# An FNet mixing and GEGLU pair on Trainium2: keeping the sums of eleven more matrix tiles between the two mixings

## The chip, the cores and the metric

The kernel runs on one core of a Trainium2 chip. The metric is the device time of one launch in microseconds (us). The kernel before takes 1598.94 us, the median of three runs between 1597.33 and 1599.78 us.

## The reference

A matrix x of 2048 rows and 512 columns (float32) passes through four residual layers: mixing, GEGLU, mixing, GEGLU. `_layernorm` has no learned weights.

```python
def _A_ref(x, dft_seq_re, dft_seq_im, dft_hid_re, dft_hid_im):
    a = jnp.einsum("bsd,ed->bse", x, dft_hid_re)
    b = jnp.einsum("bsd,ed->bse", x, dft_hid_im)
    y = jnp.einsum("ts,bse->bte", dft_seq_re, a) - jnp.einsum("ts,bse->bte", dft_seq_im, b)
    return y

def _B_ref(x, w_gate, w_up, w_down):
    return (_gelu(x @ w_gate) * (x @ w_up)) @ w_down

x = x + _A_ref(_layernorm(x, axis=-1), A_dft_seq_re, A_dft_seq_im, A_dft_hid_re, A_dft_hid_im)
x = x + _B_ref(_layernorm(x, axis=-1), B_w_gate, B_w_up, B_w_down)
x = x + _A_ref(_layernorm(x, axis=-1), A_dft_seq_re, A_dft_seq_im, A_dft_hid_re, A_dft_hid_im)
x = x + _B_ref(_layernorm(x, axis=-1), B_w_gate, B_w_up, B_w_down)
```

Both mixings use the same sequence matrices (2048 x 2048, real and imaginary), so whatever is computed from these matrices alone is the same in layer 0 and in layer 2.

## The kernel before

**Products.** Each float32 operand is split into two parts that TensorE (PE) takes: `split` (lines 156 to 160) lets ScalarE (ACT) write the rounded copy `hi` (L158) and VectorE (DVE) the rest `lo` (L160). `mm3` (lines 213 to 217) then makes three matmuls of 128x128 by 128x512: hi with hi (L215), hi with lo (L216), lo with hi (L217). To need fewer of them, the kernel multiplies 2x2 blocks by a scheme with seven products in place of eight, and such a scheme multiplies sums of blocks. For the sequence matrices the blocks of a step k are the tiles a11, a12, a21 and a22, 128x512 each (256 KB), and the sums are S1 = a21 + a22, S3 = a11 - a21, S2 = S1 - a11 and S4 = a12 - S2, by `minus` (L191) and `plus` (L198) on DVE.

**Stages.** A mixing (`mix`) treats the matrix rows in four blocks b = 0 to 3. First come the stages A11 and A12 of all blocks. Then each block has its stage S2, which runs the products of S2, S1 and S3 over the eight steps k, with S1 one step and S3 two steps behind S2 (`skewed`), then a few products with the hidden matrices, its stage S4 with the products of A22 and S4, and the rest of the hidden products. In layer 2 the blocks 2 and 3 use another form of the hidden products (`PAIRED`, tiles `wq`). The GEGLU of layer 1 follows, in two halves w, and layer 2 and 3 go the same way. The weights of the GEGLUs (`wb`, `wc`) are prepared beside the first mixing and stored to HBM by GpSimd (POOL).

**The stream of matrix tiles.** `mix_items` (lines 518 to 557) lists for every use of a matrix tile the addresses to load and the function that makes its two parts. `take` (line 356) hands the next parts to the products; `split_next` and `load_next` (lines 331 to 354) keep up to seven items split ahead and four more loaded ahead. Loads go out on SyncE's (SP's) DMA queue (L338), stores on POOL's queue. All tiles live in 98 slots of 256 KB that are handed out in the order in which they came free; a load into a slot waits until its last reader, and any store out of it, is done.

**Sums that are kept.** In layer 0 the sums of some (b, k) are stored to HBM as they are made, and in layer 2 loaded in place of the raw tiles. `KEPT` (line 50) lists which: steps 0, 1 and 2 of block 0. Two more, steps 0 and 1 of block 3, are computed and stored during layer 1 (`summed_ahead`, `SUMMED = 2`). The store is in `sums_kept`, the load in `mix_items`:

```python
def sums_kept(layer, at, sums):
    if layer == 0 and at in KEPT:
        for i, v in sums.items():
            nc.gpsimd.dma_start(wss[at][i], v)
...
for i, k in skewed(3):
    if layer and (b, k) in wss:
        raw(plain, wss[b, k][i])
    elif i == 0:
        raw(make_s2(layer, b, k), a21[k], a22[k], *(() if hold else (a11[k],)))
    else:
        raw(make_s1(k) if i == 1 else make_s3(k))
```

A step that isn't kept loads three raw tiles in stage S2 and makes three sums of them on DVE; S1 and S3 stay in their slots until their turn comes. In stage S4 it loads a12 and makes S4. A kept step loads S2, S1, S3 and S4 one by one, four tiles as well, and only splits them.

**Order.** Each engine runs its instructions in order. A scheduler orders them by a simulated timeline when the program is built, so a change at one place moves its neighbours on all engines.

Of the kernel before, what the change touches and what calls it, by code (L numbers as in the profile page):

```python
# [46 lines left out]
LATER = 3  # L47
LET = 5
SUMMED = 2
KEPT = ((0, 0), (0, 1), (0, 2))  # L50
DOWN_RUNS = ((0,0,0,0),(4,4,4,0),(4,4,4,0),2)


# [1 line left out]
def fnet_geglu(ctx: ExitStack, tc: tile.TileContext, x_in, ws, wh, wgu, wdn, wdc, whc, out):  # L55
# [240 lines left out]
    def fetched(key):  # L296
# [9 lines left out]
        (b, k): [dram.tile([P, 512], F32, name=f"ws{b}_{k}_{i}") for i in range(4)]  # L306
        for b, k in [*KEPT, *((NB - 1, k) for k in range(SUMMED))]
    }
# [87 lines left out]
# [4 lines that stand above are left out]
# [1393 lines left out]
```

## Time and profile before

| what | value |
|---|---|
| median of three runs | 1598.94 us |
| time of the profiled execution | 1598.04 us |
| span of the profiled execution | 1596.3 us |
| PE busy | 1589.5 us, 100% of the span |
| DVE busy | 1169.6 us, 73% |
| ACT busy | 891.8 us, 56% |
| POOL busy | 293.4 us, 18% |
| moved by DMA | 431.75 MB, mean 270 GB/s |

The span runs from the first to the last instruction of the profiled execution; 1.7 us of its time lie around it. Layer 0 ends at about 405 us, layer 1 at about 804 us, layer 2 at about 1174 us. In the rows of groups stand the line, the engine, the operation, the tiles written and read, the count, the busy time and the mean duration, and then the idle time of the engine just before them.

### The profile page before, as it was taken

To read this page: it belongs to the slowest core of one execution; us is meant where nothing else is said; L and a number is where in the kernel's file an instruction comes from. 1 tells how busy PE (TensorE), PEld (TensorE's weight loads), DVE (VectorE), ACT (ScalarE), POOL (GpSimd) and SP (SyncE) were. 2 spreads that over 40 slices of the span, in tenths; PEclk is the share of its full clock that TensorE was granted. 3 is DMA by queue.
4 is the path that set the end of the run, shared out by engine and by line. 5 is a ranking of instruction groups with operands and counts; after the bars stand their busy time and mean duration, and the time that the engine had idled before them with its cause. 6 is when DMAs were issued, how large, how long until landed. Compare 5 with 4: busy or idle time off the path is not lost.

```text
span 1596.3 us, 22839 instructions
## 1 busy us (share of the span) xinstructions
PE 1589.5 (100%) x6984; PEld 1310.4 (82%) x6984; DVE 1169.6 (73%) x2030; ACT 891.8 (56%) x1731; POOL 293.4 (18%) x505
## 2 busy tenths in 40 slices
PE   9999999999999999999999999999999999999999
PEld 6888888888888888888888888888878888888887
DVE  7998878888689794665879767778895557744574
ACT  8955465754767553566657535566453565333460
POOL 4122111242456101330040000011301000000000
PEclk9999999999999999999999999999999999999999
DMA  9888888997998999997895876877978958895445
GB/s 359 289 330 316 289 316 282 351 308 210 328 322 316 286 320 284 339 364 240 282 307 178 271 252 212 283 233 251 256 255 279 276 183 253 298 285 181 133 145 158
DMA packets 244058, 431.75 MB, mean 270 GB/s; under 512 B 29344, under 2 KB 68512, under 8 KB 242912
## 3 DMA queue, kind: packets, MB, share of 16 engines
q1 hardware_dynamic: 214128, 337.21, 66.0%
q0 software_dynamic: 27120, 90.99, 16.0%
q10 hardware_dynamic: 2688, 2.10, 0.4%
q8 instruction: 55, 0.90, 0.2%
q14 instruction: 67, 0.55, 0.1%
HBM read 341.31 MB, written 88.87 MB: 269 GB/s over the span
## 4 chain that ended last, share of the span: by engine, by line
PE 93%; issue 2%; DMA 2%; DVE 1%; POOL 1%; ACT 0%; SPq 0%; DVEq 0%; POOLq 0%; ACTq 0%
PE p L217 31%; PE p L216 31%; PE p L215 31%; DVE s L160 1%; DMA s<-t 1%; PE p L1016 1%; DVE s L191 0%; POOL rstd L634 0%; DMA s<-wb 0%; DMA s<-x 0%; POOL s L760 0%; DMA s<-wq 0%; DVE s L195 0%; ACT s L158 0%; POOL wb L324 0%
## 5 line engine op out<-in xcount | busy, mean ns | idle before, releaser
L216 PE MATMUL p<-s,s 128*128 128x512 f32 x2312 | 897.4, 389 | 0.4 <-DVE s L160 0.4
L217 PE MATMUL p<-s,s 128*128 128x512 f32 x2312 | 891.9, 389 | 0.3 <-DMA s<-wb 0.3
L215 PE MATMUL p<-s,s 128*128 128x512 f32 x2312 | 860.4, 389 | 0.3 <-ACT p L209 0.2
L158 ACT ACTIVATE s<-s 128x512 fp32r<-128x512 f32 (+1 forms) x855 | 481.1, 607 | 262.2 <-DVE s L191 67.7
L160 DVE TENSOR_TENSOR s<-s,s 128x512 fp32r<-128x512 f32 (+1 forms) x855 | 537.2, 663 | 114.4 <-ACT s L158 95.2
L215 PEld LDWEIGHTS p<-s,s 128*128 128x128 f32 x2312 | 434.0, 188 | 91.8 <-ACT p L209 0.9
L216 PEld LDWEIGHTS p<-s,s 128*128 128x128 f32 x2312 | 434.0, 188 | 91.2 <-DVE s L160 1.1
L217 PEld LDWEIGHTS p<-s,s 128*128 128x128 f32 x2312 | 434.0, 188 | 91.0 <-DMA s<-wb 0.8
L195 DVE TENSOR_TENSOR s<-s,p 128x512 f32<-128x512 f32 x201 | 135.9, 683 | 160.6 <-PE p L217 139.8
L191 DVE TENSOR_TENSOR s<-s,s 128x512 f32<-128x512 f32 (+1 forms) x413 | 243.9, 611 | 5.7 <-DMA s<-ws 3.3
L202 ACT ACTIVATE s<-p 128x512 f32<-128x512 f32 x232 | 134.5, 593 | 111.2 <-PE p L217 109.1
L1270 ACT ACTIVATE s<-s 128x512 f32<-128x512 f32 x84 | 52.8, 628 | 45.8 <-DVE s L195 45.5
L1270 ACT ACTIVATE s<-p 128x512 f32<-128x512 f32 x28 | 16.7, 598 | 84.1 <-PE p L217 82.4
L324 POOL DMA_DIRECT2D wb<-s x84 | 46.1, 550 | 90.7 <-ACT s L158 67.8
L634 POOL TENSOR_SCALAR rstd<-rstd 128x1 f32<-128x1 f32 x40 | 18.2, 455 | 237.9 <-ACT s L633 230.0
L160 DVE TENSOR_TENSOR s<-xwide,s 128x512 fp32r<-128x512 f32 (+1 forms) x52 | 34.8, 679 | 30.6 <-ACT s L158 30.6
L657 ACT ACTIVATE s<-s,shift,rstd 128x512 f32<-128x512 f32 x59 | 47.5, 811 | 14.6 <-DVE shift L624 8.1
L1286 DVE TENSOR_TENSOR s<-s,p 128x512 f32<-128x512 f32 x56 | 38.3, 684 | 23.4 <-PE p L217 23.4
L198 DVE TENSOR_TENSOR s<-s,s 128x512 f32<-128x512 f32 (+1 forms) x71 | 42.9, 611 | 13.1 <-DMA s<-ws 11.0
L209 ACT ACTIVATE p<-p 128x512 f32<-128x512 f32 x56 | 32.6, 584 | 24.7 <-PE p L217 24.4
L158 ACT ACTIVATE s<-xwide 128x512 fp32r<-128x512 f32 (+1 forms) x52 | 31.6, 622 | 25.7 <-DVE xwide L195 18.3
L1207 POOL DMA_DIRECT2D wc<-s x42 | 30.5, 728 | 70.2 <-ACT s L158 61.3
(104 smaller groups left out, 613.3 us busy)
## 6 DMA issues: line engine op xcount, KB each, us to landing
s<-ws SPq DMA_DIRECT2D x404, 256.0 KB, 5.2
s<-wb SPq DMA_DIRECT2D x294, 256.0 KB, 5.1
s<-wc SPq DMA_DIRECT2D x182, 256.0 KB, 4.5
wb<-s POOLq DMA_DIRECT2D x98, 256.0 KB, 4.9
s<-wh SPq DMA_DIRECT2D x84, 256.0 KB, 5.4
s<-x SPq DMA_DIRECT2D x55, 256.0 KB, 5.3
wc<-s POOLq DMA_DIRECT2D x49, 256.0 KB, 5.3
xwide<-ws SPq DMA_DIRECT2D x37, 256.0 KB, 5.4
```

The source lines that it names most:

```text
L158: newest["ACT"] = nc.scalar.activation(hi, src, AF.Copy)
L160: newest["DVE"] = nc.vector.tensor_tensor(lo, src, f32(hi), op=ALU.subtract)
L191: nc.vector.tensor_tensor(out, a, b, op=ALU.subtract)
L195: bank_read["DVE"] = nc.vector.tensor_tensor(out, a, b, op=ALU.add)
L198: nc.vector.tensor_tensor(out, a, b, op=ALU.add)
L202: bank_read["ACT"] = nc.scalar.activation(v, src, AF.Copy)
L215: nc.tensor.matmul(ps, ah, bh, start=start, stop=False, skip_group_check=True)
L216: nc.tensor.matmul(ps, ah, bl, start=False, stop=False, skip_group_check=True)
L217: newest["PE"] = nc.tensor.matmul(ps, al, bh, start=False, stop=stop, skip_group_check=True)
L324: nc.gpsimd.dma_start(a, f32(t))
L657: nc.scalar.activation(z, x, AF.Identity, bias=shift, scale=rstd)
L1270: nc.scalar.activation(t, g, AF.Gelu_apprx_tanh)
```

## The change

`KEPT` gets eleven more pairs (b, k): steps 0, 2, 4 and 6 of block 1, the same of block 2, and steps 2, 4 and 6 of block 3.

```diff
-KEPT = ((0, 0), (0, 1), (0, 2))
+KEPT = tuple((b, k) for b, ks in enumerate(((0, 1, 2), (0, 2, 4, 6), (0, 2, 4, 6), (2, 4, 6))) for k in ks)
```

In layer 0, 44 more stores of 256 KB go out on POOL's queue (L399); there the sums are made as before. In layer 2, 44 sums on DVE are no longer made, and 44 loads on SP's queue read a stored sum in place of a raw tile. The scheduler puts the instructions around them in another order.

The first place is POOL's queue at the end of block 2 and in stage S2 of block 3 of layer 0. `ws` with block, sum and step behind it is a stored sum (L399), `x_2` an output of the mixing (L285), `t_0_0` and `t_0_1` the transposed input of layer 1 (L760 fetches a part of it). Before:

```order
L285 DMA x_2_90<-s_3963 128x512
L1210 DMA wb_153<-s_3954 128x512
L285 DMA x_2_90<-s_3966 128x512
L760 DMA xwide<-t_0_0_2598 32x4x128 x4
L760 DMA s_4259<-t_0_0_2598 32x4x128
L760 DMA s_4187<-t_0_1_2599 32x4x128 x4
```

After:

```order
L399 DMA ws_4_0_177<-s_3990 128x512
L285 DMA x_2_90<-xwide 128x512
L285 DMA x_2_90<-s_4039 128x512
L285 DMA x_2_90<-s_4042 128x512
L285 DMA x_2_90<-s_4045 128x512
L399 DMA ws_2_1_174<-s_3847 128x512
L399 DMA ws_2_2_175<-s_3845 128x512
L760 DMA xwide<-t_0_0_2656 32x4x128 x4
L399 DMA ws_2_0_173<-s_3849 128x512
L760 DMA s_4306<-t_0_1_2657 32x4x128 x4
L760 DMA s_4344<-t_0_0_2656 32x4x128 x4
```

The fetches of `t_0_0` and `t_0_1` stood together behind the outputs; now stores of block 3's sums stand ahead of them and between them. Block 3 has twelve such stores: three ahead of the outputs of block 2, nine between these and the end of the fetches' stretch.

The second place is SP's queue ahead of stage S2 of block 3 in layer 2. `ws` without numbers is a raw matrix tile, `ws_2_0` and the like are stored sums (step, sum). Before:

```order
L338 DMA s_12325<-ws 128x512
L338 DMA s_12323<-ws 128x512
L338 DMA s_12327<-ws 128x512
L338 DMA s_12333<-ws_1_1_146 128x512
L338 DMA s_12364<-ws 128x512
L338 DMA s_12368<-ws 128x512
L338 DMA s_12366<-ws 128x512
L338 DMA s_12411<-ws_1_2_147 128x512
```

After:

```order
L338 DMA s_12380<-ws_2_0_173 128x512
L338 DMA s_12386<-ws_1_1_190 128x512
L338 DMA s_12392<-ws_0_2_187 128x512
L338 DMA s_12417<-ws 128x512
L338 DMA s_12421<-ws 128x512
L338 DMA s_12419<-ws 128x512
L338 DMA s_12451<-ws_2_1_174 128x512
L338 DMA s_12463<-ws_1_2_191 128x512
```

Step 2 loaded three raw tiles at once for its sums; now it loads S2 alone at that place, and S1 and S3 each follow some loads later.

## The prediction

> **What bounds the kernel now.** I read the page first, then busy times by stretch, then who waited for whom. The page's first lines say that TensorE is the bound:
>
> ```profile
> span 1596.3 us, 22839 instructions
> ...
> PE 1589.5 (100%) x6984; PEld 1310.4 (82%) x6984; DVE 1169.6 (73%) x2030; ACT 891.8 (56%) x1731; POOL 293.4 (18%) x505
> ...
> PEclk9999999999999999999999999999999999999999
> ```
>
> A busy PE need not be PE at its pace, since matmuls overlap, so the pace itself has to come from a stretch in which nothing held it up. The view of busy times in five stretches (the start, and layers 0 to 3) gives it; behind PE's busy time stands the number of matmuls, and the last three numbers are the clock, the share of the DMA engines and GB/s:
>
> ```profile
> 20.00:405.00 385.00, 385.00 (x1700) 318.75 (x1698) 324.69 (x575) 240.60 (x471) 99.49 (x168) 1.00 0.88 301
> 405.00:804.00 399.00, 398.91 (x1761) 330.10 (x1760) 297.89 (x521) 243.76 (x486) 114.19 (x185) 1.00 0.92 309
> 804.00:1174.00 370.00, 369.02 (x1626) 304.66 (x1625) 287.62 (x513) 209.19 (x408) 51.67 (x94) 1.00 0.79 251
> 1174.00:1596.30 422.30, 418.53 (x1845) 345.78 (x1843) 245.84 (x384) 184.53 (x346) 17.85 (x34) 1.00 0.72 220
> ```
>
> In layer 0 PE is busy in all of 385.00 us and does 1700 matmuls: 385.00/1700 = 0.2265 us each. At this pace the 1626 matmuls of the third row need 368.3 us of 370.0 (1.7 us lost), the 1761 of the second 398.8 us of 399.0 (0.2 us), the 1845 of the last 417.9 us of the 418.5 in which PE ran (0.6 us; the rest of that row is the end after the last matmul). So all that any change outside the start can win is 1.7 + 0.2 + 0.6 = 2.5 us, or 0.16% of 1598.94 us. The change leaves the count of matmuls, and the start, as they are. I take 0.2%, 3.2 us, as the least that a measurement of this kernel tells from no change: its three runs lie 2.45 us apart. A gain that can be told is therefore shut out by the rows, unless by a stray run.
>
> PE's own waits after the start are three, as the view of who waited for whom has them:
>
> ```profile
> PE p L216 <- DVE s L160: 0.4, 1, 0.4
> PE p L217 <- DMA s<-wb: 0.3, 1, 0.3
> PE p L215 <- ACT p L209: 0.2, 1, 0.2
> ```
>
> The latter two are the end of layer 2, where the timeline of PE shows them:
>
> ```profile
> 1167.14 0.39 PE L216 MATMUL p<-s,s 128*128 128x512 f32 x1
> 1167.86 0.50 PE L217 MATMUL p<-s,s 128*128 128x512 f32 x1 [0.33 <-DMA s<-wb]
> ...
> 1168.90 0.62 PE L215 MATMUL p<-s,s 128*128 128x512 f32 x2
> 1169.73 0.50 PE L215 MATMUL p<-s,s 128*128 128x512 f32 x1 [0.21 <-ACT p L209]
> ```
>
> From 1167.14 to 1167.86 PE does one matmul in 0.72 us, 0.49 more than its pace; from 1168.90 to 1169.73 two in 0.83 us, 0.38 more.
>
> **The change part by part: layer 2.** The 44 sums that go cost DVE what this row of groups says (L198, the pluses, has the same mean):
>
> ```profile
> L191 DVE TENSOR_TENSOR s<-s,s 128x512 f32<-128x512 f32 (+1 forms) x413 | 243.9, 611 | 5.7 <-DMA s<-ws 3.3 <-PE p L216 0.7
> ```
>
> 44 x 0.611 = 26.9 us of DVE's 287.6 in layer 2. Nearly all of that lies beside PE, which loses 1.7 us in the whole layer, so its worth is what it does at the two waits that DVE has a hand in. One is the wait for DVE L160, in stage S2 of block 0, where DVE itself is behind. Block 0's kept steps stay 0, 1 and 2, so I cost this at nothing and leave its wait where it is. The other is the wait for `wb` at 1167.86. The chain of waits leads to it through DVE:
>
> ```profile
> 1148.88 0.92 DVE s L191 x2
> ...
> 1159.77 0.60 DVE s L191
> ...
> 1161.60 0.60 DVE s L191
> 1162.20 0.28 DVE s L160
> 1162.48 5.34 DMA s<-wb
> ```
>
> DVE works without a break from 1148.88 to 1162.48, and the load of the weights starts when it is done (a slot comes free). In stage S4 of block 3 three of these subtractions go (steps 2, 4 and 6), 3 x 0.611 = 1.8 us, and nine sums went in the stage S2 just ahead. The load then starts at least 1.8 us earlier, and 0.49 us is all it has to make up. So this wait goes: -0.49 us. Next is the wait for ACT L209 behind it, a copy from one PSUM bank to another between two products; it hangs on PE's own last product and not on DVE. The bounds are 0 and -0.38; I take -0.1, nearer to no change.
>
> The loads of layer 2 stay as many, four tiles for a step, but S1 and S3 come from HBM where they lay in a slot. What a late load does is shown by the wait rows: ACT stood 19.6 us in 17 waits for matrix tiles, up to 3.8 us at once, while PE has only the one wait for a split, 0.4 us, which the sentence above ties to DVE:
>
> ```profile
> ACT s L158 <- DMA s<-ws: 19.6, 17, 3.8
> ```
>
> So up to 3.8 us of lateness at the split is hidden by the parts made ahead, and the cost is 0, with an upper bound that I take with layer 0's below.
>
> **Layer 0.** Here 44 stores are added. The twelve of block 0 in this trace give their price on POOL:
>
> ```profile
> L399 POOL DMA_DIRECT2D ws<-s x9: 539/539/542, 81.2 to 95.1; - x9
> DMA to landing us min/median/max: 5.3/6.9/7.8
> ```
>
> 44 x 0.539 = 23.7 us of POOL, which is busy in 99.5 of 385 us: hidden. What queues behind a store that waits for its sum are POOL's steps of the layer norms (L634, L635), for which ACT waits, and the fetches L760. The first row here is from the view of who waited for whom, the second from the chain of waits:
>
> ```profile
> ACT shift L636 <- POOL rstd L635: 16.4, 13, 4.9
> 361.80 18.56 issue
> ```
>
> ACT stood up to 4.9 us there, and PE has no wait for it in its three. The last of the added stores stand ahead of the 18.56 us in which the chain only passes time until POOL's next store. So I cost the queue at 0, between 0 and the 0.5 us by which a late ACT already delays PE at the end of layer 0.
>
> The bytes are the open cost. 44 x 262,144 = 11.5 MB go into layer 0. The stretches of its last two blocks, in the view of busy times:
>
> ```profile
> 254.00:287.00 33.00, 33.00 (x148) 27.32 (x147) 28.44 (x50) 17.41 (x37) 2.01 (x3) 1.00 0.79 257
> ...
> 292.00:314.00 22.00, 22.00 (x99) 18.23 (x98) 15.80 (x29) 15.57 (x33) 6.45 (x11) 1.00 1.04 394
> 314.00:330.00 16.00, 16.00 (x72) 13.28 (x71) 15.78 (x29) 10.06 (x19) 6.51 (x12) 1.00 1.04 404
> 330.00:363.00 33.00, 33.00 (x147) 27.32 (x147) 25.74 (x44) 17.57 (x33) 17.43 (x32) 1.00 1.05 268
> ...
> 368.00:390.00 22.00, 22.00 (x99) 18.23 (x98) 14.90 (x25) 8.70 (x15) 0.56 (x1) 1.00 0.59 195
> ```
>
> From 292 to 363 us the DMA engines are full; in stage S2 of block 3 (330 to 363) at only 268 GB/s, since small fetches fill them. Ahead and behind there is room (0.79, 0.59). By the order, the stores of blocks 1 and 2 fall mostly where there is room; those of block 3, twelve, fall into the full stretch, nine of them beside the fetches: 9 x 262,144 = 2.36 MB, which take 5.8 us at the 404 GB/s of the row above and 8.8 us at 268. Against this stands that PE is busy in 33.00 of 33.00 us in both the first and the fourth row, while the loads of matrix tiles took very different times to land. The issues of these two stretches:
>
> ```profile
> s<-ws SPq DMA_DIRECT2D x11, 256.0 KB, 3.3
> s<-ws SPq DMA_DIRECT2D x16, 256.0 KB, 6.8
> ```
>
> Loads that land 3.5 us later cost PE nothing. Whether they can be 5.8 to 8.8 us later still, no row shows. Since the full share means transfers that queue as early as slots allow, not that they are needed at once, I take 0 to 0.3 us here, and +0.2, and keep 2.3 to 5.3 us (5.8 and 8.8 less the 3.5 shown) as the other end.
>
> [...]
>
> **Sum.** -0.49 - 0.1 + 0.2 = -0.4 us. The profiled execution would go from 1598.04 to 1597.6 us; it lies 0.9 us below the median of the runs, so the forecast is 1598.94 - 0.4 = 1598.5 us: no change that can be told.
>
> **Rivals.** The first, slower: the nine stores come between the loads of stage S2 of block 3 in layer 0 and the loads between 330 and 363 us land late. For it speaks the full share and landing times of 6.8 us; against it 3.5 us of shown patience, the 3.8 us at ACT, and the emptier stretch behind. It decides from the point at which a load lands later than the parts made ahead last: then PE waits 2.3 to 5.3 us, and the time is 1598.5 + 2.3 to 5.3 = 1600.8 to 1603.8 us, some 1602.5 us. [...] I give it 18 in 100.
>
> The second: the stall at the end of layer 2 does not go, because the load of `wb` waits for a slot that another reader holds, or a like wait arises elsewhere, where the scheduler has put things in another order. The chain's `issue` pieces and the late ACT at the end of layer 0 speak for it; the three subtractions taken from an unbroken run of DVE against it. It gives 1598.9 to 1599.5 us: 22 in 100.
>
> The third, faster: all losses of layer 2 and the hand-over go, 1.7 + 0.2 us: 1597.0 us. Against it stands that block 0's wait is not touched. 8 in 100; even that lies within 0.2%. The forecast itself has 52 in 100.
>
> **How the numbers follow.** The forecast, the second and the third rival, 82 in 100 together, all lie within 0.2%; for stray measurements and waits that I don't see I take 3 from them to the faster side and 4 to the slower. Of the first rival's 18, 7 stay below 1602.1 us, 3.2 above the time before. That gives faster 0.03, within 0.2% 82 - 7 + 7 = 0.82, slower 11 + 4 = 0.15. The range starts at 1596.8 us, just under the third rival, and goes to 1602.0 us, into the first rival, so that some 15 in 100 are left out above and 5 below.
>
> **What would show it.** Right: in the profile after, layer 2's DVE is busy 27 us less, L191 and L198 have 44 instructions less, L399 has 56, the wait of PE for `wb` at the end of layer 2 is gone, and PE is busy in all of the stretch from 330 to 363 us though the DMA share stays above 1. Wrong: PE waits for DVE L160 or ACT L158 in that stretch, with ACT L158 waiting for `ws` ahead of it, or PE's matmuls per us in layer 0 fall below 1700 in 385 us. If the time rises while layer 0 has no gap, the reordering of layer 2 is the cause.

## The result, and the profile after

The changed kernel is slower: 1611.78 us, the median of four runs (1607.72 to 1613.55), against 1598.13 us of the kernel before in the same runs. The ratio is 1.0082, with a 95% interval of 1.006 to 1.0105. The prediction's 1598.5 us and its range up to 1602.0 us are both missed.

The profiled execution of the changed kernel is the shortest of its four, 1607.72 us with a span of 1606.0 us; it shows 9.7 us more than the profiled execution before. The other three, 1611.7 us and longer, have no trace, so some 4 us of the difference are not placed by what follows. Their mean granted clocks are 0.999, 0.997 and 0.998, for 0.999 in the profiled one: the first is 4.0 us longer at the same mean clock, so a lower clock of TensorE is not all of it.

The page after, span and busy times:

```profile
span 1606.0 us, 22882 instructions
...
PE 1591.1 (99%) x6984; PEld 1310.9 (82%) x6984; DVE 1144.5 (71%) x1986; ACT 891.1 (55%) x1731; POOL 325.0 (20%) x549
```

DVE has the 44 instructions less (1986 for 2030) and is 25.1 us less busy. PE's busy time grew by only 1.6 us while the span grew by 9.7: where PE waited can't be seen here, but it can in the count of matmuls by stretch. Busy times by stretch, layers 0 and 2 (columns as in the prediction):

```profile
20.00:405.00 385.00, 378.94 (x1665) 311.97 (x1664) 318.58 (x562) 234.83 (x457) 124.68 (x204) 1.00 0.93 326
...
804.00:1174.00 370.00, 366.87 (x1618) 303.21 (x1617) 261.32 (x468) 206.32 (x402) 51.45 (x94) 1.00 0.79 250
```

Layer 0 had 1700 matmuls in its 385 us; now it has 1665. At 0.2265 us each, 35 x 0.2265 = 7.9 us are lost there, where nothing was lost before. Layer 2 needs 370/0.2265 = 1633.6 matmuls to lose nothing; it had 1626 (1.7 us lost) and has 1618 (3.5 us). The DVE time of layer 2 fell from 287.62 to 261.32 us and bought nothing. Layer 1 is about as before (1758 matmuls for 1761). The share of the DMA engines in layer 0 rose from 0.88 to 0.93.

Who PE waited for, after:

```profile
PE p L215 <- ACT s L158: 4.5, 3, 2.5
PE p L216 <- DVE s L160: 2.6, 3, 1.5
...
PE p L215 <- DMA s<-wh: 1.3, 1, 1.3
PE p L215 <- ACT p L209: 1.2, 2, 0.7
```

The first two rows are waits for split tiles (L158 makes `hi`, L160 `lo`). Before, PE had one of that kind, of 0.4 us; now there are six, together 7.1 us. The row for `wh`, the hidden matrices, is new too: PE stands 1.3 us for such a load in layer 0, at 377 us, where it had no such wait before. The row for `wb` is gone. The timeline of PE shows the first place, in layer 0, and the largest, in layer 2:

```profile
310.55 0.39 PE L217 MATMUL p<-s,s 128*128 128x512 f32 x1
311.69 1.66 PE L215 MATMUL p<-s,s 128*128 128x512 f32 x6 [0.76 <-ACT s L158]
314.89 0.50 PE L216 MATMUL p<-s,s 128*128 128x512 f32 x1 [1.54 <-DVE s L160]
...
1137.95 0.39 PE L217 MATMUL p<-s,s 128*128 128x512 f32 x1
1140.83 0.49 PE L215 MATMUL p<-s,s 128*128 128x512 f32 x1 [2.49 <-ACT s L158]
1141.97 0.50 PE L216 MATMUL p<-s,s 128*128 128x512 f32 x1 [0.65 <-DVE s L160]
```

From 1137.95 to 1141.97 PE does two matmuls in 4.02 us: 3.6 us lost at one place in stage S2 of block 3, which is all that layer 2 loses. In layer 0 it is several places; 310.55 to 314.89 is the first (seven matmuls in 4.34 us, 2.8 us lost), the rest lie between 342 and 378 us. The stretches that answer to those of before:

```profile
254.00:287.00 33.00, 33.00 (x148) 27.32 (x147) 26.64 (x47) 15.98 (x29) 5.56 (x10) 1.00 0.93 331
...
330.00:363.00 33.00, 32.54 (x144) 26.61 (x143) 21.82 (x35) 12.59 (x22) 20.78 (x39) 1.00 1.04 321
```

The stretch at 254 us, in which the prediction saw room (0.79, 257 GB/s), is nearly full. In stage S2 of block 3 PE now has 144 matmuls in 33 us for 147, and the issues of that stretch show how the loads fare: those of matrix tiles take 8.4 us to landing where it was 6.8 us, those of `wh` 9.8 us where it was 5.8 us:

```profile
s<-ws SPq DMA_DIRECT2D x17, 256.0 KB, 8.4
...
s<-wh SPq DMA_DIRECT2D x4, 256.0 KB, 9.8
```

### The profile page after: what moved, and what is told of

Its sections match the earlier page's. It is cut to its first block, busy times and chain, and to the rows that moved or that the text cites. A ratio compares the mean times of both kernels' runs of the same rounds, so it can differ in the third digit from the quotient of the medians.

```text
span 1606.0 us, 22882 instructions
## 1 busy us (share of the span) xinstructions
PE 1591.1 (99%) x6984; PEld 1310.9 (82%) x6984; DVE 1144.5 (71%) x1986; ACT 891.1 (55%) x1731; POOL 325.0 (20%) x549
## 4 chain that ended last, share of the span: by engine, by line
PE 95%; DMA 1%; DVE 1%; ACT 1%; issue 1%; POOL 1%; SPq 0%; ACTq 0%; DVEq 0%; POOLq 0%
PE p L216 31%; PE p L215 31%; PE p L217 31%; DMA s<-ws 1%; PE p L1016 1%; DVE s L160 1%; POOL rstd L634 0%; PE p L1699 0%; DMA s<-wh 0%; DMA s<-x 0%; DVE s L191 0%; ACT s L158 0%; DVE s L195 0%; ACT p L209 0%; ACT s L631 0%
## 5 line engine op out<-in xcount | busy, mean ns | idle before, releaser
L158 ACT ACTIVATE s<-s 128x512 fp32r<-128x512 f32 (+1 forms) x855 | 482.3, 608 | 296.6 <-DVE s L191 75.4
L160 DVE TENSOR_TENSOR s<-s,s 128x512 fp32r<-128x512 f32 (+1 forms) x855 | 535.4, 661 | 135.3 <-ACT s L158 113.5
L191 DVE TENSOR_TENSOR s<-s,s 128x512 f32<-128x512 f32 (+1 forms) x382 | 223.1, 603 | 11.2 <-DMA s<-ws 7.3
L634 POOL TENSOR_SCALAR rstd<-rstd 128x1 f32<-128x1 f32 x40 | 22.8, 569 | 215.4 <-ACT s L633 209.8
L160 DVE TENSOR_TENSOR s<-xwide,s 128x512 fp32r<-128x512 f32 (+1 forms) x52 | 34.9, 680 | 24.0 <-ACT s L158 23.8
L746 DVE STREAM_TRANSPOSE wide<-s 128x512 f32<-128x512 f32 x31 | 21.9, 708 | 40.0 <-ACT s L657 35.6
L198 DVE TENSOR_TENSOR s<-s,s 128x512 f32<-128x512 f32 (+1 forms) x61 | 36.2, 596 | 19.1 <-DMA s<-ws 17.2
L209 ACT ACTIVATE p<-p 128x512 f32<-128x512 f32 x56 | 32.6, 584 | 23.7 <-PE p L217 22.9
L1286 DVE TENSOR_TENSOR s<-s,s 128x512 f32<-128x512 f32 x56 | 38.5, 688 | 1.3
```

The lines of the kernel that those rows point to most:

```text
L158: newest["ACT"] = nc.scalar.activation(hi, src, AF.Copy)
L160: newest["DVE"] = nc.vector.tensor_tensor(lo, src, f32(hi), op=ALU.subtract)
L191: nc.vector.tensor_tensor(out, a, b, op=ALU.subtract)
L1286: nc.vector.tensor_tensor(t, t, v, op=ALU.mult)
```

## The experiments

Two theories stood at first: the cost is that of the added stores in layer 0 (bytes, or slots that a stored sum holds longer), or that of layer 2's new order of loads. All runs are in one table first; what was expected of each and the rows that decide follow. "Lost" is worked out as above, from the matmuls n in the profiled execution's rows of stretches: (1700 - n) x 0.2265 us for 20 to 405 us, (1633.6 - n) x 0.2265 us for 804 to 1174 us. It belongs to one execution, the median and the ratio to all; the ratio compares all runs of both kernels and need not be the quotient of the medians. The stretches are the same for all kernels, so in one that is late by 8 us the last 8 us of layer 2 lie outside. stores_only's 0 leaves out a stall of 0.38 us at 1176 us for that reason.

| kernel | median us | ratio to before, 95% interval | n, lost us in layer 0 | n, lost us in layer 2 |
|---|---|---|---|---|
| before (profiled) | 1597.66 to 1598.13 | 1 | 1700, 0 | 1626, 1.7 |
| after | 1611.78 | 1.0082, 1.006 to 1.0105 | 1665, 7.9 | 1618, 3.5 |
| stores_only | 1605.16 | 1.0043, 1.0028 to 1.0058 | 1665, 7.9 | 1635, 0 |
| loads_only | 1603.64 | 1.0034, 1.0021 to 1.0048 | 1700, 0 | 1600, 7.6 |
| block3_only | 1605.45 | 1.0045, 1.003 to 1.0061 | 1688, 2.7 | 1597, 8.3 |
| quarter_bytes | 1601.89 | 1.0025, 1.0015 to 1.0034 | 1682, 4.1 | 1626, 1.7 |
| wide_on_pool | 1598.16 | 1.0004, 0.9995 to 1.0012 | 1700, 0 | 1633, 0.1 |
| block1_only | 1596.99 | 0.9995, 0.9986 to 1.0004 | 1700, 0 | 1629, 1.0 |
| block2_only | 1599.5 | 1.001, 1.0001 to 1.002 | 1698, 0.5 | 1631, 0.6 |
| blocks12_only | 1599.91 | 1.0013, 1.0004 to 1.0022 | 1687, 2.9 | 1632, 0.4 |
| tiny_bytes | 1598.73 | 1.0007, 0.9998 to 1.0016 | 1699, 0.2 | 1628, 1.3 |
| rows64 | 1598.28 | 1.0003, 0.9993 to 1.0012 | 1688, 2.7 | 1624, 2.2 |
| rows120 | 1608.27 | 1.0061, 1.0046 to 1.0076 | 1672, 6.3 | 1627, 1.5 |
| all_wide_on_pool | 1605.87 | 1.0046, 1.0033 to 1.0058 | 1662, 8.6 | 1630, 0.8 |
| block1_wide_on_pool | 1597.09 | 1.0002, 0.9992 to 1.0011 | 1699, 0.2 | 1632, 0.4 |
| before_wide_on_pool | 1597.4 | 0.9998, 0.9989 to 1.0006 | 1698, 0.5 | 1626, 1.7 |

### One half of the change alone

stores_only keeps the stores of layer 0; layer 2 loads the raw tiles as before, and has the order of before. The first of two like places:

```diff
-                    if layer and (b, k) in wss:
+                    if layer and (b, k) in wss and (b, k) not in KEPT[3:]:
...
```

> Makes and stores the 44 added sums in layer 0 as the changed kernel does, in the same order on every engine there, but layer 2 loads the raw tiles and makes the sums as before (the stored sums are not used). Theory A (two separate costs: the stores cost PE about 7.6 us between 305 and 380 us, the loads of the sums cost about 3.7 us in stage S2 of block 3 of layer 2): PE's gaps in layer 0 come back at about 7 to 9 us, layer 2 has no gap over 1 us, time 1604 to 1608 us. Rival B (all of it comes from layer 2 or from a shift of the whole program): within 2 us of before. Rival C (the profile's gaps in layer 0 are chance): gaps in layer 0 at other places or none.

loads_only has no added store, and the order of before in layer 0; layer 2 has the order and the number of loads of the changed kernel, but it loads raw tiles in place of the stored sums and leaves these sums out.

```diff
-        if layer == 0 and at in KEPT:
+        if layer == 0 and at in KEPT[:3]:
...
-                    if layer and (b, k) in wss:
+                    if layer and (b, k) in KEPT[3:]:
+                        raw(plain, (a11, a21, a22)[i][k])
+                    elif layer and (b, k) in wss:
...
```

> Layer 0 as before, without the 44 stores; layer 2 in the order of the changed kernel, but where that loads a stored sum this one loads a raw tile of the same size and splits it, so the sums of those eleven steps are left out. Theory A: no gap in layer 0, one of 3 to 4 us near 1128 us (1138 less the 10 of layer 0), and the wait for wb at the end of layer 2 gone: time 1599 to 1602 us. Rival B (stores and loads matter only together, since the stored sums come from HBM later than raw tiles): equal to before within 1 us. Rival D (fewer sums on DVE help where nothing is stored): 0.5 to 1.5 us under before.

The rows of layers 0 and 2 of stores_only, then those of loads_only:

```profile
20.00:405.00 385.00, 379.06 (x1665) 311.92 (x1664) 317.98 (x562) 235.98 (x457) 124.70 (x204) 1.00 0.92 326
...
804.00:1174.00 370.00, 370.00 (x1635) 306.45 (x1634) 289.20 (x516) 208.00 (x404) 51.80 (x94) 1.00 0.80 252
```

```profile
20.00:405.00 385.00, 385.00 (x1700) 318.89 (x1699) 324.89 (x575) 240.75 (x471) 102.35 (x168) 1.00 0.87 301
...
804.00:1174.00 370.00, 366.07 (x1600) 301.88 (x1599) 256.67 (x460) 205.19 (x400) 51.19 (x94) 0.99 0.78 249
```

Each half loses in its own layer and nothing in the other's. The medians add up: 1605.16 - 1597.66 = 7.5 us and 1603.64 - 1597.66 = 6.0 us make 13.5 us, and the whole change costs 1611.78 - 1598.13 = 13.65 us. So there are two costs, and neither theory by itself is enough. loads_only lies above the 1599 to 1602 us that were expected; part of that is a lower clock behind its stall, shown at the end.

### The layer 2 half: the head of SP's queue

In loads_only and in the changed kernel the stall stands at the same place, stage S2 of block 3. The timeline of SP's queue there, first before, then loads_only (start, time from the first to the last issue, count; L908 of the kernel before is L912 in loads_only):

```profile
1105.68 5.24 SPq L338 DMA_DIRECT2D s<-ws  x5
1111.22 1.94 SPq L908 DMA_DIRECT2D wide<-x  x4
1113.82 5.10 SPq L338 DMA_DIRECT2D s<-ws  x3
```

```profile
1104.79 3.94 SPq L338 DMA_DIRECT2D s<-ws  x4
1111.53 0.88 SPq L912 DMA_DIRECT2D wide<-x  x2
1112.49 0.44 SPq L338 DMA_DIRECT2D s<-ws  x1
1112.98 0.96 SPq L912 DMA_DIRECT2D wide<-x  x2
1114.04 2.12 SPq L338 DMA_DIRECT2D s<-ws  x3
```

Before, SP came to the loads of `wide` just as the store of `t_0_1` landed, and stood 0.2 us. With the new order it comes to them at 1108.73, and stands until 1111.53. SP's wait in loads_only at this place:

```profile
SPq L912 <- DMA t<-wide: 2.7, 1, 2.7
```

`wide` has one buffer, and the store of `t_0_1` out of it has not landed. The raw tiles behind, from which S1 of a step that isn't kept is made, then go out together with 1 MB of `wide` and the fetches of the transposed input, and DVE stands 8.4 us for one of them (its row is below). wide_on_pool is loads_only with the four loads of `wide` on POOL's queue, where they come behind the same store and two groups of fetches:

```diff
-            moved(pair_wide[n], xs[layer, paired[n]], lambda v, rows: nc.sync.dma_start(v, rows))
+            moved(pair_wide[n], xs[layer, paired[n]], lambda v, rows: (nc.gpsimd if n else nc.sync).dma_start(v, rows))
```

> As loads_only (no added stores; layer 2 loads raw tiles at the places of the stored sums, and the sums of those eleven steps are left out of the output), with one edit: the four loads of wide at L908 in layer 2 go out on POOL's queue, behind the store of t_0_1 and two groups of fetches, in place of SP's. loads_only waited there on SP for 3.0 us (1108.5 to 1111.5), with three raw tiles for the sums of stage S2 of block 3 queued behind. Theory (the head of SP's queue): these raw tiles go out some 3 us earlier, the stall of PE at 1131 to 1136 (3.9 us and about 2.2 us at half clock in loads_only) falls below 1 us, and the median lies between 1597.5 and 1600. Rival (the burst of wide, fetches and raw tiles that comes together at 1110 to 1125, whatever their queue): the stall stays above 2.5 us and the median between 1602 and 1604.

The edit moves hardly anything else: PE, ACT and all of layer 0 keep the order of loads_only. The stretches from 1120 us on, of loads_only and then of wide_on_pool:

```profile
1120.00:1130.00 10.00, 10.00 (x46) 8.28 (x45) 1.59 (x3) 2.05 (x5) 5.42 (x10) 1.00 1.07 287
...
1130.00:1136.00 6.00, 3.19 (x12) 1.99 (x11) 5.72 (x10) 2.12 (x4) 4.36 (x8) 0.86 0.99 253
1136.00:1142.00 6.00, 6.00 (x16) 4.74 (x17) 1.90 (x3) 4.28 (x9) 0.55 (x1) 0.57 0.78 227
```

```profile
1120.00:1130.00 10.00, 10.00 (x45) 8.27 (x45) 9.18 (x16) 4.12 (x7) 4.79 (x9) 1.00 1.05 239
1130.00:1136.00 6.00, 6.00 (x27) 4.67 (x26) 2.97 (x5) 3.28 (x6) 3.35 (x7) 1.00 1.06 249
1136.00:1142.00 6.00, 6.00 (x28) 4.99 (x27) 5.85 (x11) 4.36 (x9) 2.79 (x6) 1.00 1.05 295
```

From 1120 to 1130 us DVE does 3 instructions in loads_only (1.59 us busy) and 16 in wide_on_pool. In the next 6 us PE has 12 matmuls for 27: that is the stall. In the 6 us behind it PE is busy throughout and has 16 for 28, at a granted clock of 0.57; that is the lower clock. In wide_on_pool PE loses nothing. The median falls from 1603.64 to 1598.16 us, inside the theory's 1597.5 to 1600, and the stall is gone, so the rival as it was put, that the burst costs as much on any queue, is out.

How much of the gain is the wait at the head of the queue and how much the burst is not shown. SP's row for these raw tiles in wide_on_pool (that of loads_only is the last one above):

```profile
1105.06 8.10 SPq L338 DMA_DIRECT2D s<-ws  x6
```

DVE's instruction that waits for the last of them, in loads_only and then in wide_on_pool:

```profile
1128.41 0.69 DVE L198 TENSOR_TENSOR s<-s,s 128x512 f32<-128x512 f32 x1 [8.42 <-DMA s<-ws]
```

```profile
1120.82 0.69 DVE L198 TENSOR_TENSOR s<-s,s 128x512 f32<-128x512 f32 x1 [5.01 <-DMA s<-ws]
```

SP has issued them by 1113.16 in place of 1116.16 us, 3.0 us earlier, but DVE starts 7.6 us earlier. So less than half is SP's wait; in the rest the tiles land faster (7.66 us from the last issue to DVE's start, 12.25 us in loads_only), now that they are issued ahead of most of the megabyte of `wide` and not behind it. The edit changes both at once. It also shows that 5.0 us of DVE's waiting cost PE nothing here.

The same edit was tried on the whole change and on the kernel before.

> The changed kernel whole, with the four loads of wide (L908) of layer 2 on POOL's queue. Theory (two costs, independent of each other): the stall of layer 2 (3.6 us in the profile of the changed kernel, more with half-clock matmuls behind it) goes, the stalls of layer 0 stay as in stores_only: 1603 to 1606. Rival (what is late in layer 0 shifts the rest, so that the layer 2 stall of the whole kernel has another cause than in loads_only): 1609 to 1612.

It gives 1605.87 us, that is stores_only's 1605.16 and no more: the layer 2 half is gone from the whole kernel as well, and the layer 0 half stays: the two costs add up. It takes 5.9 us off the changed kernel's 1611.78.

> The kernel before with the loads of wide on POOL's queue, nothing else: does that edit do anything by itself? In the kernel before SP reached these loads at 1111.0 us, just as the store of t_0_1 had landed, so SP hardly waited there, and the theory expects no difference over 1 us: 1597 to 1598.5. If the burst of wide and fetches on SP costs something in the kernel before too, 1594.5 to 1596.5.

No difference (0.9998, 0.9989 to 1.0006), as expected: in the kernel before SP stood there for 0.2 us alone.

### The layer 0 half: which stores, and bytes or order

block3_only, block1_only, block2_only and blocks12_only add only some of the eleven steps to the kernel before. block3_only's edit; the others list the steps of their blocks:

```diff
-KEPT = ((0, 0), (0, 1), (0, 2))
+KEPT = ((0, 0), (0, 1), (0, 2), (3, 2), (3, 4), (3, 6))
```

> Keeps only the three added steps of block 3 (12 of the 44 stores). Theory of the prediction's first rival (the nine to twelve stores beside the fetches in the full stretch from 292 to 363 us are what hurts): gaps of 4 to 7 us between 305 and 380 us, time 1602 to 1608 us. Rival (what hurts is the sum of all stores from 150 us on, which uses up the room ahead of the full stretch): gaps under 2 us in layer 0. Layer 2's gap in block 3 should appear in both, 3 to 4 us, if it comes from block 3's loads.

Block 3 loses 2.7 us in layer 0, at 360 to 374 us, between the two expectations (4 to 7 us, and under 2 us). PE's waits there are these, from the view of who waited for whom between 20 and 405 us:

```profile
PE p L215 <- DMA s<-wh: 1.4, 1, 1.4
PE p L215 <- ACT p L209: 0.3, 1, 0.3
```

Neither is a wait for a split tile. So the 2.7 us fall within the prediction's first rival by their size (2.3 to 5.3 us), but block 3's stores alone do not make its mechanism. Most of what this kernel loses lies in layer 2, 8.3 us, nearly all at 1132 to 1143 us, where SP stands 3.1 us for the store of `t_0_1` ahead of `wide` as in the changed kernel. The time is in the expected range for that reason, not for the one given.

> Only the four steps of block 1 are added (16 stores, 16 loads of sums). If the cost in layer 0 is the bytes of block 2's stores (209 to 287 us) and of block 3's (323 to 371 us), each where it falls, there is no stall beyond those of before at 310 to 376 us, and in layer 2 no stall over 1 us at 1131 to 1141, since block 3's order there is that of before: 1596.5 to 1599.5. If any added store costs about alike (44 cost 7.5 us, 0.17 us each), 16 of them give 1600.5 to 1602.

> Only the four steps of block 2 are added (16 stores, 16 loads of sums). If block 2's stores make the stalls at 310 to 316 us (2.9 us in the changed kernel) by themselves, these are there again with 1.5 to 3 us and those at 342 to 376 us are not: 1599 to 1602. If the stall at 310 needs block 1's stores as well, or is block 3's, there is nothing beyond before in layer 0: 1596.5 to 1599. In layer 2 no stall over 1 us at 1131 to 1141 is expected, since block 3 loads raw tiles there as before.

> The eight steps of blocks 1 and 2 are added, block 3's are not (32 stores, 32 loads of sums). block1_only and block2_only had no stall at 310 to 316 us. Theory (the lead of the loads is used up by all the bytes together): the two blocks together do make one there, 1 to 3 us, and none at 342 to 376 us: 1599 to 1602. Rival (the stall at 310 to 316 us comes from block 3's steps, by the order around them): none there, 1596 to 1599. Layer 2 loads raw tiles for block 3 as before, so no stall over 1 us at 1131 to 1141.

Block 1 alone costs nothing that can be told, block 2 alone 0.1% with 0.5 us lost in layer 0, a little above what was expected for the case without a stall at 310 us. Both together lose 2.9 us, nearly all at 311 to 315 us, as the changed kernel does. The stretch from 160 to 200 us of block2_only, then of blocks12_only:

```profile
160.00:200.00 40.00, 40.00 (x178) 33.12 (x177) 33.48 (x56) 19.67 (x37) 7.02 (x11) 1.00 0.83 294
```

```profile
160.00:200.00 40.00, 40.00 (x179) 33.10 (x178) 33.98 (x57) 19.35 (x35) 13.99 (x24) 1.00 1.02 380
```

Block 1's stores turn the stretch from 160 to 200 us from 0.83 to 1.02 full. At 292 to 314 us the share is 1.04 in both, at 395 and 396 GB/s, as it was before. So one block's stores fit into what is left of the DMA engines, two do not. The cost comes some 150 us behind the first of the stores (159 us) and some 25 us behind the last (287 us), in the stretch that was full before. What carries it there was not followed.

The next kernels are stores_only with smaller stores: 128 of 512 columns in quarter_bytes, 8, 64 or 120 of 128 rows in tiny_bytes, rows64 and rows120. In all of them the sums are made and stored as often as in stores_only. The edit of tiny_bytes, beside that of stores_only:

```diff
-                nc.gpsimd.dma_start(wss[at][i], v)
+                n = 8 if at in KEPT[3:] else P
+                nc.gpsimd.dma_start(wss[at][i][:n], v[:n])
```

> As stores_only, but each added store writes only the first 128 of 512 columns, so 2.9 MB in place of 11.5 MB; POOL issues as many and the slots are held until the store lands. The scheduler orders layer 0 a little otherwise. If bytes on the DMA engines are the cost: gaps of layer 0 fall to under 2 us, time within 2 us of before. If POOL's queue or the slots held behind a store are the cost: at least two thirds of the gaps of stores_only stay, 1603 us or more.

> As stores_only (layer 2 as before), with each of the 44 added stores writing only 8 of 128 rows, 16 KB in place of 256 KB; the order of the instructions differs a little from both stores_only and quarter_bytes. Theory (bytes): with 0.7 MB in place of 11.5 MB nothing is left in layer 0, no stall over 0.7 us at 300 to 380 us: 1596.5 to 1599. Rival (slots held and queue places: every sum still keeps its slot until its store on POOL's queue has read it): the stall at 370 us stays with 1 to 2.5 us, as in quarter_bytes, and the median lies between 1600 and 1602.5.

> As stores_only, with each of the 44 added stores writing 120 of 128 rows (94% of the bytes, 10.8 MB); the scheduler makes of it an order that differs from stores_only in some 40 places on DVE and SP each, from about 170 us on. Theory (bytes): the stalls in layer 0 are of the same size though not in the same places, 5 to 10 us against 8.4 in stores_only, and the median lies between 1602.5 and 1607. Rival (an unlucky order): under 3 us of stalls and 1597 to 1601.

> As stores_only, with each of the 44 added stores writing 64 of 128 rows (5.8 MB). Theory (bytes): between quarter_bytes (3.0 us of stalls in layer 0) and stores_only (8.4): 3 to 8 us, and 1601.5 to 1605.5. Rival (an unlucky order): no relation to the bytes; under 2 us, or more than stores_only, would speak for it.

The row of layer 0 in tiny_bytes, in rows64 and in rows120:

```profile
20.00:405.00 385.00, 385.00 (x1699) 318.61 (x1698) 324.49 (x575) 239.75 (x468) 128.00 (x211) 1.00 0.88 302
```

```profile
20.00:405.00 385.00, 382.36 (x1688) 316.41 (x1687) 322.01 (x569) 235.90 (x461) 129.04 (x208) 1.00 0.89 313
```

```profile
20.00:405.00 385.00, 380.12 (x1672) 313.14 (x1671) 322.28 (x568) 236.47 (x457) 122.24 (x205) 1.00 0.92 326
```

With 0.7 MB in place of 11.5 the cost is gone, though the 44 stores still stand on POOL's queue (POOL is as busy, 128.00 us). So neither POOL's time nor the queue places cost anything that can be told. rows120 has 94% of the bytes in another order: it has no stall at 311 us, but one of 2.3 us at 340 us and others behind, 6.3 us in all, and 1608.27 us, above the 1602.5 to 1607 that were expected. Two orders with nearly all the bytes cost 7.5 and 10.3 us, so one unlucky order is not the cause; where the stalls fall and how large they are changes with the order.

In between the size does not follow the bytes. rows64, with half of them, has a median of 1598.28 us, below the 1601.5 to 1605.5 expected, and less than quarter_bytes with a quarter of them: its 1601.89 us and 4.1 us fit neither of its expectations (within 2 us of before, or 1603 us and more). Up to half the bytes the cost is between 0.03% and 0.25%, at 94% and more between 0.43% and 0.61%. In the profiled executions of these two PE waits in layer 0 for a load of `wh` and not for a split tile, rows64 first, then quarter_bytes:

```profile
PE p L215 <- DMA s<-wh: 2.6, 1, 2.6
```

```profile
PE p L215 <- DMA s<-wh: 2.2, 1, 2.2
```

SP's queue from 355 to 374 us, before and then rows64:

```profile
362.89 6.92 SPq L338 DMA_DIRECT2D s<-wh  x12
```

```profile
362.41 2.13 SPq L338 DMA_DIRECT2D s<-wh  x3
364.63 0.86 SPq L338 DMA_DIRECT2D s<-ws  x2
365.58 6.65 SPq L338 DMA_DIRECT2D s<-wh  x8
```

Before, and in tiny_bytes, the twelve loads of `wh` go out in a row and PE does not wait. In every kernel with this wait a load or two of matrix tiles stand among them; blocks12_only and all_wide_on_pool have some there too and no such wait. So the order has a hand in this stall but does not make it alone. What rows64 and quarter_bytes do show is that with up to half of the bytes no split tile comes late in layer 0. The rest of quarter_bytes' 4.1 us is the clock: behind the stall it was granted 0.72 from 373 to 379 us, and eight intervals between matmuls are longer by 0.2 us each, 1.6 us in all. rows64's profiled execution, which lost 2.7 us at full clock, was one of its longer ones (1600.53 us).

A sum that is stored also holds its slot until the store is done: from issue to landing the full stores of the changed kernel took 5.7 us in the median. How much shorter this is with a smaller store is not shown. Between 20 and 405 us SP's waits have no row for a store of a sum in the changed kernel and in stores_only. They have one in the kernels with smaller stores: 5.5 us in three waits in tiny_bytes, where PE loses nothing by it, 4.9 us in quarter_bytes, 4.0 in rows64 and 3.0 in rows120. That speaks against slots as the cost of the whole change; a kernel with the bytes but without the holding was not tried.

### A version that beats both

Block 1's steps alone were free, so block1_wide_on_pool joined them with the edit of L908.

> block1_only with the loads of wide on POOL's queue: a try at a version that beats both. block1_only still had stalls of 0.66 us at 906 us and 0.50 us at 1169 us; wide_on_pool had neither. If these go, 1595.5 to 1596.8; if they are block 1's own, 1596.5 to 1598.

It loses 0.6 us in both layers, where the kernel before loses 1.7. The stall at 906 us is gone, the one at the end of layer 2 is not. The median is 1597.09 us, a ratio of 1.0002 (0.9992 to 1.0011): no difference that can be told. No kernel tried here beats the kernel before.

## Why the prediction was wrong, step by step

- **What bounds the kernel: held.** The pace of 0.2265 us and the count of matmuls placed the losses of the profiled executions, and the sign that was named for being wrong, fewer than 1700 matmuls in layer 0, came (1665). That at most 2.5 us can be won also held: wide_on_pool loses nothing in layer 0 and 0.1 us in layer 2 and is not measurably faster.
- **DVE's 26.9 us are worth nothing: held.** 261.32 us for 287.62 in layer 2, and no gain.
- **The wait for `wb` goes: not shown.** The row is gone, but it is gone in stores_only too, which has layer 2 as before. It comes and goes without the change. The other wait there, 0.38 us for ACT L209, is gone in every kernel that doesn't make block 3's sums in layer 2 and stayed in stores_only, so there the change did gain something, more than the 0.1 us taken.
- **The loads of layer 2 cost 0: failed, 6.0 us.** The step counted the loads (still four a step) and the patience at the split (up to 3.8 us). It did not ask what else stands on SP's queue. Both orders quoted of SP's queue end several loads ahead of those of `wide`, and that issue, which waits for a store, with raw tiles behind it, is the cost. The patience was misread as well. The 3.8 us were waited in layer 0, at 213 us; in layer 2 the longest such wait was 2.3 us. And the time that an engine stands for a part is not how late the part comes for PE, as the changed kernel's layer 2 shows: here ACT stood 10.6 us and PE lost nothing, while 8.45 us of DVE's, up to 1134.6 us, were too much.

```profile
947.49 1.15 ACT L158 ACTIVATE s<-s 128x512 fp32r<-128x512 f32 x2 [10.59 <-DMA s<-ws]
```

- **The bytes of layer 0 cost 0.2 us: failed, 7.5 us.** The cost comes with the bytes (tiny_bytes is free of it), as in the first rival, given 18 in 100, but even that rival's size (2.3 to 5.3 us) was too small. It looked only at block 3's nine stores, which fall beside the fetches; block 3's stores alone lose 2.7 us, and not by late matrix tiles. Blocks 1 and 2 were put down as falling "mostly where there is room", and lose 2.9 us together, by late split tiles at 311 us. That makes 5.6 of the 7.9 us; the rest comes only with all stores at once (one execution each). And the patience of 3.5 us was read from a median of landing times in two stretches: it says that such loads were early enough there, not that any load may be that late. It was also lateness that the loads of block 3 had already, so it could not be taken off what the stores would add. Block 3's loads landed 1.6 us later in the median than before (8.4 for 6.8), and PE stood all the same. The prediction has no term for the loads of `wh`, which made 1.3 us of it.
- **The queue of POOL costs 0: held.** tiny_bytes shows it, within its interval (0.9998 to 1.0016).
- **Chances.** Two costs at once were not among the cases. The second rival named "a like wait elsewhere" in layer 2, but at 0.4 to 1 us, not 6.

## What to carry to other kernels

Before adding transfers, look at what the DMA engines have left over the whole stretch ahead, not only where the transfer falls: block 1's stores were free, those of blocks 1 and 2 together cost 2.9 us, 25 us behind the last of them. When loads move, list everything on the issuing queue, find the entry that waits for something other than a free slot, and ask what is urgent behind it; moving that one entry to another queue took back 5.5 us here. A landing time that was harmless in one place is no allowance for another (a median of 6.8 us cost PE nothing here, with one of 8.4 us it stood), and neither is the time that an engine stood idle for a load (10.6 us of ACT's cost PE nothing, 8.45 us of DVE's were too much).

## What was not expected of the hardware

In loads_only the stall cost 2.0 us more than its own length, because PE came back at a lower clock. The timeline of PE there:

```profile
1131.79 0.39 PE L217 MATMUL p<-s,s 128*128 128x512 f32 x1
1134.63 0.80 PE L215 MATMUL p<-s,s 128*128 128x512 f32 x1 [2.46 <-ACT s L158]
1135.78 0.80 PE L216 MATMUL p<-s,s 128*128 128x512 f32 x1 [0.35 <-DVE s L160]
1136.37 0.63 PE L217 MATMUL p<-s,s 128*128 128x512 f32 x1
...
1140.64 0.63 PE L215 MATMUL p<-s,s 128*128 128x512 f32 x1
```

From 1136.37 to 1140.64 matmuls follow each other at 0.43 us in place of 0.2265, and the row of the stretch 1136 to 1142 above gives a granted clock of 0.57. These ten intervals cost 10 x 0.2 = 2.0 us on top of the stall. Within it the clock is 0.50 (1135 to 1141 us). By the rows for 1130 to 1136 and 1136 to 1142 us, with 0.86 and 0.57, it lasted 6.8 us, an estimate that takes the rest of these rows at full clock. Behind the like stall of block3_only the clock falls as well (0.74 from 1132 to 1145 us), and in layer 0 behind stalls of quarter_bytes and of all_wide_on_pool (0.96 each from 363 to 405 us). In the profiled execution of the changed kernel the like stall (1137.95 to 1141.97) has no such row behind it (1.00 from 1142 to 1148 us), and rows64 had 2.8 us lost between two matmuls at 370 us without it (1.00 from 363 to 390 us).

The length of the stall does not tell the two cases apart: PE's longest idle time in it was 2.46 us in loads_only and 2.49 us in the changed kernel. What brings the clock down is not shown by any run here. The lower clock may be part of why the changed kernel's other three runs are 4 us longer than the profiled one, but they have no trace, so this is only argued.
